# Replanning the hand-written engine order of a fused RWKV-6 attention and squared-ReLU feed-forward kernel

## The chip, the cores and the metric

The kernel runs on one core of one Trainium2 chip. A core has five engines that run side by side, each with its own queue of instructions that it takes strictly in order: TensorE (PE, matrix multiplications; its weight loads are shown apart, as PEld), VectorE (DVE), ScalarE (ACT), GpSimd (POOL) and SyncE (SP), which here only issues transfers to 16 DMA engines. Engines wait for each other by semaphores. The metric is the device time of one execution in microseconds; smaller is better.

## The reference

The inputs are r, k, v and w for 4 batches, 8 heads, 768 positions and 48 channels in float32, a vector u per head, and two matrices w_in (384 x 2048) and w_out (2048 x 384). For each batch and head a 48 x 48 state is carried over the positions, and the result goes through a feed-forward layer with a squared ReLU:

```
for t in range(S):
    cur = np.einsum('bhd,bhe->bhde', u[None] * kt, vt)
    y[:, :, t] = np.einsum('bhd,bhde->bhe', rt, state + cur)
    state = wt[:, :, :, None] * state + np.einsum('bhd,bhe->bhde', kt, vt)
x = np.ascontiguousarray(attn_out.transpose(0, 2, 1, 3)).reshape(B * S, H * D)
h = x @ w_in
r = np.maximum(h, 0.0)
g = r * r
return (g @ w_out).astype(np.float32)
```

## The kernel before

The recurrence is done in chunks of 128 positions: 4 batches of 6 chunks make 24 *steps*. Two steps (256 tokens) make a *block* of the feed-forward layer, of which there are 12. Every piece of work is a small function, and a text of *words*, `order`, says in which sequence the functions are called. The scheduler is told to leave all five engines alone (`tc.manual_schedule` at the end), so the sequence of the words is the sequence of instructions on each engine: a word that waits holds up every later word of its engine, and the relative place of words on different engines matters only through their data.

The words, with the step (or block) as the first number:

- SP: `ld:s:w`, `ld:s:k`, `ld:s:r`, `ld:s:v` load 192 KB each of a step (L67); `ld:h:I` and `ld:h:O` load slice h of w_in (L90) and of w_out (L96), eight slices of 384 KB each; `store:i:mt` stores 128 rows of the result (L345). Eight DMA semaphores are used in turn, and a transfer waits for the one eight places before it. A load also waits until its buffer is free: each of w, v and the pair r, k has seven buffers.
- ScalarE: `lw` takes the logarithm of w, `exp` (L197, or L199 and L200) exponentiates the cumulated sums, `rw` is a reciprocal of w, `v` casts v, `ac` gives the decay over a chunk, `xt` copies the transposed result into `xT`, `rl:i:g` is the ReLU of one m1 word (L321), `os` the scaled copy of a finished output tile (L341).
- VectorE: `rd` (L207) multiplies r and k by the decays, `rkt` (L220) copies their transposes, `pm` (L239) and `pmh` (L247) mask the scores, `ts` (L269) adds to the state, `q` reduces (L180), `ysb` (L291) adds up y, `gt:i:q` (L329) squares two relu tiles.
- POOL: `ku`, `qp`, `vq`, `kw`, `sn`, products of the recurrence (L172, L176, L184, L164, L273).
- TensorE: `cum` (L190) cumulates the logarithms, `tr` (L216) transposes, `p` (L234) makes the scores of one step or of two, `su` (L255 to L260) the state update, `y` (L281, L286) the output, `yt` (L297) its transposes. `m1:i:g:b` (L312) is 6 matmuls of 256 columns of x times slice g of w_in into bank b. `m2:i:mt:q:b` (L336) is 4 matmuls of 384 columns with slices 2q and 2q+1 of w_out. `warm:n:b` (L363) is n matmuls whose result nobody reads, fillers. `last` (L351) is half of the last output tile.
- `cast:i:g:j` and `cast:o:g:j` (L104) cast slice 2g+j of w_in or w_out to bfloat16, on ScalarE where g is even and on VectorE where it is odd. So w_in slices 6 and 7 are cast on VectorE (`cast:i:3:0`, `cast:i:3:1`), and m1 words with g = 7 need slice 7.

PSUM gives four banks to m1, m2, the second step's scores and the fillers (b is 0 to 3), two to `cp`, one to `tr` and one to `y`. A word that takes a bank waits until the bank's last reader is done: `rl` for m1, `os` for m2, `pmh` for scores.

Of the kernel before, what the change touches and what calls it, by code (L numbers as in the profile page):

```python
# [16 lines left out]
def kernel(  # L17
# [110 lines left out]
    warm = consts.tile([C, 512], BF16)  # L128
# [236 lines left out]
    def ld_(n, x):  # L365
# [15 lines left out]
        rd:4 m1:0:3:2 xt:3 ld:6:I m1:0:1:0 kw:5 rl:0:3 ld:7:I cum:5 tr:4 exp:5 gt:0:1 ld:0:O m1:1:0:3 ld:1:O sn:3 rkt:4
        ld:2:O m1:1:2:1 v:4 ld:3:O q:4 rl:0:1 m1:1:3:2 ld:4:O rd:5 vq:4 ld:5:O rl:1:2 m1:1:1:0 ld:5:v cast:i:2:0 su:4
        gt:0:0 p:4 ac:4 cast:i:2:1 m1:0:4:1 rl:1:3 ts:4 m1:1:4:2 cast:i:3:0 pm:4 sn:4 tr:5 rl:1:0 warm:1:3 qp:5 ld:6:w
        rl:1:4 rkt:5 m1:1:5:3 rl:1:1 y:4 gt:1:1 p:5 rl:1:5 cast:i:3:1 m1:1:6:2 cast:o:0:0 gt:1:0 m1:1:7:0 rl:0:4 gt:1:2
        m1:0:6:3 rl:1:6 cast:o:0:1 m1:0:5:1 rl:0:6 ysb:4 m1:0:7:2 rl:0:5 pm:5 ld:6:O yt:4 m2:0:1:0:3 rl:1:7 m2:0:0:0:1
        cast:o:1:0 cast:o:1:1 ld:7:O m2:1:1:0:0 gt:0:2 cast:o:2:0 m2:1:1:1:0 ld:6:k q:5 m2:0:1:1:3 cast:o:2:1 v:5 ld:7:w
        vq:5 xt:4 y:5 m2:0:1:2:3 rl:0:7 ysb:5 ld:6:r lw:6 m2:1:1:2:0 gt:0:3 rw:6 yt:5 cum:6 gt:1:3 m2:0:0:1:1 xt:5
        cast:o:3:0 m2:0:0:2:1 ld:7:k m1:2:0:2 exp:6 cast:o:3:1 ku:6 m2:1:1:3:0 ld:7:r rl:2:0 m2:0:0:3:1 kw:6 lw:7 ld:6:v
        m2:0:1:3:3 rw:7 os:0:0 rd:6 m1:2:4:2 ld:8:k os:1:1 ku:7 os:0:1 cum:7 ld:8:w tr:6 exp:7 m1:2:5:1 rkt:6 kw:7
        ld:9:w m1:2:1:0 v:6 qp:7 m2:1:0:0:3 rd:7 ld:7:v rl:2:1 qp:6 q:7 rl:2:4 tr:7 ld:8:r m1:2:6:0 rl:2:5 rkt:7 ku:8  # L390
        ld:8:v p:6 lw:8 q:6 m1:2:2:2 pm:6 vq:6 ld:9:k su:6 m1:2:3:1 ac:6 rw:8 vq:7 ld:9:r ts:6 m2:1:0:1:3 rl:2:2 gt:2:0
        p:7 v:7 ld:10:k sn:6 m1:2:7:2 pm:7 lw:9 y:6 qp:8 rl:2:6 m2:1:0:2:3 ld:11:k rl:2:3 ysb:6 m2:1:0:3:3 kw:8 ld:10:r
# [12 lines left out]
        m2:4:1:0:3 ld:16:v pmh:11:1 rw:15 ld:15:r sn:10 cum:13 y:10 v:11 pmh:11:0 m2:4:0:0:1 rw:14 ku:14 rkt:12 rl:4:7
        m2:4:1:1:3 store:1:0 ysb:10 qp:13 ld:17:v v:12 m2:4:0:1:1 exp:13 ld:16:r yt:10 gt:4:3 y:11 m2:4:1:2:3 ku:15
        xt:10 ysb:11 ld:17:r m2:4:0:2:1 rd:13 kw:14 yt:11 m2:4:1:3:3 xt:11 q:13 ld:16:w kw:15 cum:14 v:13 su:12 q:12
        m2:4:0:3:1 ac:12 ld:17:w exp:14 qp:15 ts:12 m1:5:2:0 ld:18:k tr:13 os:4:1 qp:14 rd:14 m1:5:4:2 os:4:0 store:2:1
        rl:5:2 rkt:13 m1:5:0:3 vq:13 store:2:0 ld:18:w p:12:1:0 sn:12 rl:5:0 store:4:0 su:13 rl:5:4 ld:19:w pm:12
        m1:5:3:3 vq:12 ld:18:r ac:13 lw:16 m1:5:1:2 ku:16 rl:5:3 ts:13 y:12 cum:15 pmh:13:1 rw:16 tr:14 sn:13 v:14  # L410
        m1:5:6:3 ld:19:k ysb:12 rl:5:1 kw:16 m1:5:5:0 rkt:14 pmh:13:0 yt:12 m1:5:7:2 ld:20:w xt:12 gt:5:0 y:13 exp:15
        su:14 store:4:1 gt:5:1 m2:5:1:0:1 ld:19:r ac:14 ysb:13 rl:5:6 m2:5:1:1:1 ld:20:r ts:14 rl:5:5 m2:5:0:0:3 rd:15
        sn:14 rl:5:7 yt:13 m2:5:0:1:3 xt:13 gt:5:3 cum:16 lw:18 tr:15 gt:5:2 exp:16 m1:6:0:0 q:14 m1:6:2:2 v:15 rkt:15
        qp:16 m2:5:1:2:1 rl:6:0 rd:16 m2:5:1:3:1 rl:6:2 vq:14 su:15 q:15 lw:17 p:14:0:2 ku:17 os:5:1 q:16 m2:5:0:2:3
        ac:15 store:5:1 pmh:15:0 lw:19 ku:18 ld:20:k m2:5:0:3:3 rw:17 pm:14 ld:21:r m1:6:1:1 v:16 kw:17 ld:18:v os:5:0
        m1:6:3:0 ts:15 rl:6:1 qp:17 y:14 rl:6:3 ld:19:v m1:6:4:3 ysb:14 vq:15 cum:17 pmh:15:1 tr:16 rl:6:4 ld:21:w ku:19
        m1:6:5:1 exp:17 rkt:16 y:15 store:3:0 gt:6:0 yt:14 ld:22:w rl:6:5 m1:6:6:0 sn:15 ysb:15 ld:23:w xt:14 m1:6:7:2
        rd:17 qp:18 yt:15 m2:6:0:0:3 ld:21:k xt:15 gt:6:1 cum:18 rl:6:6 su:16 gt:6:2 m1:7:2:1 ac:16 rw:18 ld:20:v q:18
        m1:7:3:0 rl:6:7 kw:18 ts:16 m2:6:0:1:3 ld:22:k rl:7:2 gt:6:3 m1:7:0:2 exp:18 store:5:0 q:17 tr:17 ld:21:v
        m2:6:0:2:3 rw:19 qp:19 rd:18 ld:23:k rl:7:3 m1:7:1:1 rkt:17 kw:19 rl:7:0 m2:6:0:3:3 ld:22:r rl:7:1 gt:7:1  # L420
        p:16:0:2 os:6:0 sn:16 m1:7:6:1 pm:16 lw:21 ld:22:v vq:16 tr:18 rl:7:6 m1:7:4:3 ld:23:r gt:7:0 cum:19 vq:17
        m1:7:7:1 rl:7:4 pmh:17:1 v:17 y:16 vq:18 m1:7:5:3 v:18 ysb:16 ku:21 lw:20 m2:7:0:0:2 pmh:17:0 rl:7:5 m2:7:0:1:2
        rkt:18 ku:20 exp:19 m2:6:1:0:0 gt:7:2 yt:16 m2:6:1:1:0 qp:20 xt:16 rd:19 m2:7:1:0:3 rw:21 kw:21 su:18 y:17 ac:18
        cum:20 rl:7:7 m2:7:1:1:3 ysb:17 lw:22 ts:18 m2:7:1:2:3 rw:20 gt:7:3 yt:17 v:20 m2:7:0:2:2 sn:18 q:20 xt:17
        m2:6:1:2:0 q:19 kw:20 exp:20 tr:19 m2:6:1:3:0 rkt:19 vq:19 m2:7:1:3:3 os:6:1 rd:20 qp:21 m2:7:0:3:2 v:19
        store:6:1 ld:23:v os:7:1 p:18:1:0 ku:22 q:21 os:7:0 m1:8:0:3 pm:18 store:7:0 m1:8:2:2 store:6:0 rl:8:0 su:19
        pmh:19:1 m1:8:6:3 ac:19 rl:8:2 ts:19 y:18 cum:21 pmh:19:0 m1:8:3:0 exp:21 ysb:18 tr:20 m1:8:1:2 rl:8:3 rkt:20
        y:19 rw:22 gt:8:1 yt:18 m1:8:7:1 rl:8:6 kw:22 ysb:19 xt:18 m1:8:4:0 rd:21 rl:8:1 sn:19 yt:19 m1:8:5:3 xt:19
        gt:8:0 cum:22 rl:8:4 su:20 m1:9:0:2 ac:20 rl:8:5 ts:20 m2:8:0:0:0 exp:22 gt:8:2 m1:9:1:3 sn:20 tr:21 rl:8:7
# [48 lines left out]
```

## Time and profile before

| what | value |
|---|---|
| median of 6 runs | 194.89 us (193.75 to 195.54) |
| the profiled execution | 194.91 us, span 193.0 us |
| PE busy | 184.1 us (95% of the span) |
| DVE, ACT, POOL busy | 144.2, 132.2, 110.7 us |
| DMA | 30.20 MB, q1 67.2% of 16 engines' span |
| loads, median from issue to landing | 3.7 to 3.9 us (w, k, r, v), 5.6 and 7.0 us (w_in, w_out) |

The span runs from the first to the last instruction; what lies around it makes up the rest of the execution's time. The second part of the page cuts the span into 40 slices and gives the busy share of each in tenths, with the granted TensorE clock:

```profile
PE   6899789899999999999999999999999999999993
PEclk9999999999999999999999999999999999999999
DMA  6999998999999979997898959990050000004032
```

The DMA engines are full from the first microseconds to beyond the middle, and nearly still in the last quarter. TensorE has gaps in the first quarter and at the very end only. A busy share of TensorE counts filler matmuls too, so the first quarter has to be looked at by line.

### The profile page before, as it was taken

The page shows a single profiled execution, that of the slowest core. Times are in us where ns is not written, and L with a number is a line of the kernel's source. Part 1 is how long each engine was busy: PE and PEld are TensorE (multiplying, and loading weights), DVE is VectorE, ACT ScalarE, POOL GpSimd, SP SyncE. Part 2 cuts the span into 40 slices and gives each one's busy share as a digit, 9 for nine tenths or more (in the row PEclk, how much of TensorE's full clock was granted, in tenths as well). Part 3 has the DMA queues.
Part 4 walks back from the last instruction along what each step waited for, and adds up shares of the span by engine and source line. Part 5 has one row for each costly group of instructions (what it writes and reads, how often), then busy time and mean ns, then how long its engine had stood idle before and what let it go on. Part 6 is the DMA issues. An engine that isn't in the chain of part 4 may idle for free.

```text
span 193.0 us, 4976 instructions
## 1 busy us (share of the span) xinstructions
PE 184.1 (95%) x1962; PEld 136.7 (71%) x1966; DVE 144.2 (75%) x211; ACT 132.2 (68%) x284; POOL 110.7 (57%) x128
## 2 busy tenths in 40 slices
PE   6899789899999999999999999999999999999993
PEld 2355548676687787787688787886688787688763
DVE  3586987895679889789979959988888858744310
ACT  3554379788777876899487876877768677247530
POOL 7488556401789749949994595795905950130000
PEclk9999999999999999999999999999999999999999
DMA  6999998999999979997898959990050000004032
GB/s 122 202 208 193 288 263 234 311 332 251 197 189 195 209 156 219 179 248 157 189 238 190 202 128 211 195 198 11 11 155 0 0 3 0 5 0 163 3 122 82
DMA packets 108840, 30.20 MB, mean 156 GB/s; under 512 B 100497, under 2 KB 108818, under 8 KB 108818
## 3 DMA queue, kind: packets, MB, share of 16 engines
q1 hardware_dynamic: 108818, 29.89, 67.2%
q8 instruction: 15, 0.25, 0.5%
q14 instruction: 7, 0.06, 0.1%
HBM read 25.17 MB, written 4.72 MB: 155 GB/s over the span
## 4 chain that ended last, share of the span: by engine, by line
PE 77%; SPq 14%; DMA 3%; DVE 2%; issue 2%; DVEq 0%
PE mm L336 31%; PE mm L312 28%; SPq L67 11%; PE tr L216 4%; SPq L90 4%; DMA w_st<-in_moe_w_in_dram 3%; PE y L281 2%; PE cp L234 2%; PE tr L297 2%; PE cp L190 2%; PE y L286 1%; PE tr L255 1%; PE mm L351 1%; PE mm L234 1%; PE tr L260 1%
## 5 line engine op out<-in xcount | busy, mean ns | idle before, releaser
L312 PE MATMUL mm<-xT,wi_sb 128*128 128x256 bf16 x576 | 73.9, 273 | 0.8 <-ACT rl L321 0.5
L336 PE MATMUL mm<-wo_sb,gt 128*128 128x384 bf16 x368 | 68.3, 326 | 0.0
L321 ACT ACTIVATE rl<-mm 128x512 f16<-128x512 f32 x96 | 55.0, 598 | 18.8 <-PE mm L312 15.5
L312 PEld LDWEIGHTS <-wi_sb 128*128 128x128 bf16 x576 | 53.8, 98 | 10.3 <-issue 1.0
L336 PEld LDWEIGHTS <-gt 128*128 128x128 bf16 x368 | 34.6, 98 | 18.1
L329 DVE TENSOR_TENSOR gt<-rl 128x1024 bf16<-128x1024 f16 x48 | 38.7, 819 | 8.6 <-ACT rl L321 8.6
L184 POOL TENSOR_TENSOR vq<-v_raw,q 128x384 f32<-128x384 f32 x24 | 21.6, 905 | 17.6 <-DVE q L180 17.6
L172 POOL TENSOR_TENSOR ku<-rk_raw,u_bc 128x384 f32<-128x384 f32 x24 | 25.6, 1070 | 8.4 <-DMA rk_raw<-in_k_dram 5.0
L164 POOL TENSOR_TENSOR rk_raw<-rk_raw,rw 128x384 f32<-128x384 f32 x19 | 19.3, 1019 | 15.6 <-ACT rw L160 12.4
L207 DVE TENSOR_TENSOR rdec_buf<-rk_raw,cp 128x768 bf16<-128x768 f32 x24 | 22.8, 948 | 6.1 <-ACT cp L197 2.9
L273 POOL TENSOR_TENSOR S<-t_state,a_c 128x384 bf16<-128x384 f32 x20 | 18.1, 907 | 15.5 <-DVE t_state L269 13.7
L176 POOL TENSOR_TENSOR qprod<-rk_raw,ku 128x384 f32<-128x384 f32 x24 | 25.2, 1057 | 2.6 <-DVE q L180 1.8
L220 DVE COPY rkT<-tr 128x1024 bf16<-128x1024 bf16 x24 | 16.5, 687 | 10.0 <-PE tr L216 9.7
L239 DVE TENSOR_TENSOR pmT<-cp,tri_strict 128x1024 bf16<-128x1024 f32 x16 | 19.5, 1218 | 1.5 <-PE cp L234 1.5
L291 DVE TENSOR_TENSOR y_sb<-vq,y 128x384 bf16<-128x384 f32 x24 | 13.2, 550 | 8.5 <-PE y L286 4.7
L300 ACT COPY xT<-tr 128x384 bf16<-128x384 bf16 x24 | 11.5, 481 | 11.1 <-PE tr L297 10.9
L156 ACT ACTIVATE lw_buf<-w_raw 128x384 bf16<-128x384 f32 x24 | 12.6, 524 | 5.0 <-DMA w_raw<-in_w_dram 5.0
L363 PE MATMUL mm<-warm 128*128 128x512 bf16 x47 | 14.2, 411 | 1.5 <-DVE warm L129 1.3
L216 PE MATMUL tr<-ident,rdec_buf 128*128 128x128 bf16 x192 | 14.6, 219 | 0.1
L341 ACT ACTIVATE o_sb<-mm 128x384 f32<-128x384 f32 x23 | 11.0, 492 | 5.1 <-PE mm L336 4.9
L216 PEld LDWEIGHTS <-rdec_buf 128*128 128x128 bf16 x192 | 12.6, 98 | 2.5 <-issue 0.7
L168 ACT CAST v_bf<-v_raw 128x384 bf16<-128x384 f32 x24 | 12.0, 508 | 2.4 <-DMA v_raw<-in_v_dram 2.4
(59 smaller groups left out, 197.4 us busy)
## 6 DMA issues: line engine op xcount, KB each, us to landing
w_raw<-in_w_dram SPq DMA_DIRECT2D x24, 192.0 KB, 3.8
rk_raw<-in_k_dram SPq DMA_DIRECT2D x24, 192.0 KB, 3.7
rk_raw<-in_r_dram SPq DMA_DIRECT2D x24, 192.0 KB, 3.9
v_raw<-in_v_dram SPq DMA_DIRECT2D x24, 192.0 KB, 3.9
out_dram<-o_sb SPq DMA_DIRECT2D x23, 192.0 KB, 2.7
w_st<-in_moe_w_in_dram SPq DMA_DIRECT2D x8, 384.0 KB, 5.6
w_st<-in_moe_w_out_dram SPq DMA_DIRECT2D x8, 384.0 KB, 7.0
out_dram<-o_sb SPq DMA_DIRECT2D x2, 96.0 KB, 1.6
```

The lines of the kernel that those rows point to most:

```text
L67: nc.sync.dma_start(out=dst, in_=src[b, :, c * C:(c + 1) * C, :].rearrange("h c d -> c h d"))
L164: nc.gpsimd.tensor_mul(k_s, k_s, tiles.pop(("rw", s))[:])
L172: nc.gpsimd.tensor_mul(ku[:], raw["rk", s][:, 1], u_bc[:])
L176: nc.gpsimd.tensor_mul(qp[:], raw["rk", s][:, 0], tiles.pop(("ku", s))[:])
L184: nc.gpsimd.tensor_mul(vq[:], raw["v", s][:], tiles.pop(("q", s))[:, :, None].to_broadcast([C, H, D]))
L207: nc.vector.tensor_mul(rdec[:, :, :, 0:D], raw["rk", s][:], tiles.pop(("cs", s))[:, :, 0:DM].rearrange("p a (h d) -> p a h d", h=H))
L216: nc.tensor.transpose(ps_tr[:, i, p, :], rdec[:, i, 2 * p:2 * p + 2, :], ident[:])
L239: nc.vector.tensor_mul(pmT[:].rearrange("p e a t -> p (e a) t"), tiles.pop(("p", s))[:].rearrange("p e (a t) -> p (e a) t", a=HP), tri_str ...
L312: nc.tensor.matmul(ps1[:, j * width:(j + 1) * width], wi_sb[:, kk, n * 128:(n + 1) * 128], xT[:, kk, s0 * C:s0 * C + width], start=(kk == ...
L321: nc.scalar.activation(tiles["rl", i, q][:, j], tiles.pop(("m1", i, g))[:], AF.Relu, scale=RS)
L329: nc.vector.tensor_mul(tiles["gt", i][:, 4 * q:4 * q + 4, :].rearrange("p a b -> p (a b)"), rl, rl)
L336: nc.tensor.matmul(tiles["m2", i, mt][:, 0:DM], gt[:, n, mt * 128:(mt + 1) * 128], wo_sb[:, n, :], start=(n == 0), stop=(n == NT - 1))
```

## The change

The text `order` is replaced. No function, tile, buffer count or instruction changes, apart from bank numbers. Every word of before is there again, except fillers: 17 filler words with 51 matmuls become 15 with 43. The words stand in another sequence on all five engines. Its description names a model with measured loads and a smaller DMA ring; neither a load time nor a ring size is written in the code, they belong to the planner that made the order. What the diff looks like, cut to the beginning, the stretch where step 19's w is loaded and used, and the end:

```diff
--- before.py
+++ after.py
@@ -370,75 +370,75 @@
     order = """
-        ld:0:w ld:0:k warm:6:0 ld:0:r ld:0:u ld:1:w lw:0 ld:1:k cum:0 warm:2:1 ld:1:r exp:0 ub rd:0 ld:0:v lw:1 warm:1:2
-        ld:2:w uc cum:1 ku:0 tr:0 ld:2:r exp:1 warm:8:3 rkt:0 qp:0 ld:1:v rd:1 v:0 ku:1 ld:2:k q:0 p:0 su:0 lw:2 vq:0
-        pm:0 ld:2:v warm:5:0 ac:0 ld:3:w ts:0 y:0 cum:2 sn:0 tr:1 exp:2 ld:3:k warm:4:1 rkt:1 qp:1 v:1 ld:4:k rd:2 su:1
-        ku:2 warm:1:2 ac:1 v:2 ld:3:r q:1 p:1 warm:2:3 ts:1 vq:1 lw:3 ld:3:v pm:1 tr:2 sn:1 warm:3:0 ld:0:I rkt:2 qp:2
-        ld:1:I cum:3 warm:3:1 exp:3 ld:2:I ysb:0 ku:3 ld:4:w yt:0 y:1 rd:3 ld:4:r xt:0 warm:1:2 qp:3 su:2 ysb:1 v:3 p:2
-        warm:3:3 ac:2 ts:2 q:3 yt:1 warm:2:0 xt:1 ld:5:w pm:2 vq:3 cast:i:0:0 tr:3 warm:1:1 sn:2 rkt:3 y:2 q:2 p:3
-        ld:3:I su:3 cast:i:1:0 vq:2 ld:5:k pm:3 m1:0:0:2 ld:4:I ac:3 ku:4 m1:0:2:3 lw:4 ts:3 rl:0:0 cum:4 ld:4:v ysb:2
-        qp:4 warm:2:0 exp:4 y:3 cast:i:0:1 yt:2 rl:0:2 ld:5:r warm:6:1 ysb:3 lw:5 ld:5:I xt:2 cast:i:1:1 rw:5 yt:3 ku:5
-        rd:4 m1:0:3:2 xt:3 ld:6:I m1:0:1:0 kw:5 rl:0:3 ld:7:I cum:5 tr:4 exp:5 gt:0:1 ld:0:O m1:1:0:3 ld:1:O sn:3 rkt:4
-        ld:2:O m1:1:2:1 v:4 ld:3:O q:4 rl:0:1 m1:1:3:2 ld:4:O rd:5 vq:4 ld:5:O rl:1:2 m1:1:1:0 ld:5:v cast:i:2:0 su:4
-        gt:0:0 p:4 ac:4 cast:i:2:1 m1:0:4:1 rl:1:3 ts:4 m1:1:4:2 cast:i:3:0 pm:4 sn:4 tr:5 rl:1:0 warm:1:3 qp:5 ld:6:w
-        rl:1:4 rkt:5 m1:1:5:3 rl:1:1 y:4 gt:1:1 p:5 rl:1:5 cast:i:3:1 m1:1:6:2 cast:o:0:0 gt:1:0 m1:1:7:0 rl:0:4 gt:1:2
-        m1:0:6:3 rl:1:6 cast:o:0:1 m1:0:5:1 rl:0:6 ysb:4 m1:0:7:2 rl:0:5 pm:5 ld:6:O yt:4 m2:0:1:0:3 rl:1:7 m2:0:0:0:1
...
-        rl:5:2 rkt:13 m1:5:0:3 vq:13 store:2:0 ld:18:w p:12:1:0 sn:12 rl:5:0 store:4:0 su:13 rl:5:4 ld:19:w pm:12
...
-        ac:15 store:5:1 pmh:15:0 lw:19 ku:18 ld:20:k m2:5:0:3:3 rw:17 pm:14 ld:21:r m1:6:1:1 v:16 kw:17 ld:18:v os:5:0
-        m1:6:3:0 ts:15 rl:6:1 qp:17 y:14 rl:6:3 ld:19:v m1:6:4:3 ysb:14 vq:15 cum:17 pmh:15:1 tr:16 rl:6:4 ld:21:w ku:19
-        m1:6:5:1 exp:17 rkt:16 y:15 store:3:0 gt:6:0 yt:14 ld:22:w rl:6:5 m1:6:6:0 sn:15 ysb:15 ld:23:w xt:14 m1:6:7:2
-        rd:17 qp:18 yt:15 m2:6:0:0:3 ld:21:k xt:15 gt:6:1 cum:18 rl:6:6 su:16 gt:6:2 m1:7:2:1 ac:16 rw:18 ld:20:v q:18
...
-        m1:11:0:0 gt:10:3 rl:11:2 m2:10:0:0:3 rl:11:0 m2:10:0:1:3 m1:11:1:1 m2:10:0:2:3 rl:11:1 m1:11:5:0 gt:11:0
-        m1:11:3:1 rl:11:5 m2:10:0:3:3 rl:11:3 gt:11:2 m2:11:0:0:0 os:10:0 gt:11:1 m2:10:1:2:2 store:10:0 m2:10:1:3:2
-        m2:11:0:1:0 os:10:1 m2:11:0:2:0 store:10:1 store:8:1 m2:11:0:3:0 os:11:0 store:11:0 last:11:1:1:0 last:11:1:2:1
+        ld:0:w ld:0:k warm:6:0 ld:0:u ld:0:r ld:1:w lw:0 ld:0:v cum:0 ld:1:r ub exp:0 ld:1:k warm:2:1 rd:0 lw:1 ld:2:w
+        tr:0 uc cum:1 rkt:0 ld:1:v v:0 ku:0 warm:1:2 exp:1 su:0 ld:2:k warm:8:3 ac:0 rd:1 ku:1 ld:2:r lw:2 ts:0 ld:0:I
+        qp:1 p:0 tr:1 pm:0 v:1 ld:2:v qp:0 warm:3:0 rkt:1 ld:3:w cum:2 sn:0 warm:1:1 exp:2 q:1 su:1 ku:2 warm:6:2 ld:3:r
+        ac:1 rd:2 vq:1 ld:3:k q:0 p:1 warm:2:3 ts:1 vq:0 ld:1:I pm:1 tr:2 qp:2 y:0 lw:3 ld:4:w warm:2:0 v:2 rkt:2 cum:3
+        ld:5:w warm:3:1 exp:3 ysb:0 ku:3 q:2 yt:0 y:1 ld:3:v xt:0 rd:3 warm:1:2 sn:1 su:2 ld:2:I ac:2 ysb:1 p:2
+        cast:i:0:0 qp:3 warm:2:3 ts:2 ld:4:k pm:2 yt:1 vq:2 warm:2:0 xt:1 ld:3:I lw:4 tr:3 ld:4:v sn:2 q:3 m1:0:0:1 lw:5
+        rkt:3 vq:3 v:3 y:2 rl:0:0 p:3 cast:i:0:1 ld:4:r su:3 pm:3 cast:i:1:0 m1:0:1:2 ku:4 ld:5:k rl:0:1 m1:0:2:3 ysb:2
+        ac:3 cum:4 rw:5 ts:3 ld:5:r y:3 exp:4 cast:i:1:1 yt:2 warm:1:0 sn:3 ld:4:I ysb:3 m1:0:3:1 xt:2 v:4 yt:3 rd:4
+        qp:4 ld:5:I warm:3:2 xt:3 ld:6:I rl:0:2 ld:7:I ku:5 cum:5 q:4 tr:4 ld:0:O rl:0:3 ld:1:O m1:1:0:0 gt:0:0 exp:5
+        ld:2:O m1:1:2:2 kw:5 ld:3:O rkt:4 ld:5:v m1:1:3:3 rl:1:2 gt:0:1 su:4 qp:5 cast:i:2:0 m1:1:1:1 rd:5 ac:4 m1:1:4:2
+        vq:4 rl:1:3 ts:4 p:4 rl:1:0 cast:i:2:1 m1:0:4:3 sn:4 rl:1:1 pm:4 ld:4:O tr:5 cast:i:3:0 ld:5:O m1:1:5:0 gt:1:1
+        ld:6:w rl:0:4 m1:0:6:1 gt:1:0 rl:1:4 y:4 m1:0:5:3 rl:1:5 rkt:5 m1:1:6:2 cast:i:3:1 rl:0:5 ysb:4 rl:0:6 m1:0:7:0
+        cast:o:0:1 cast:o:0:0 m1:1:7:3 gt:1:2 p:5 rl:0:7 m2:1:1:0:1 ld:6:O gt:0:2 cast:o:1:0 ld:7:O yt:4 cast:o:1:1
+        m2:0:0:0:0 ld:7:w rl:1:6 q:5 m2:1:1:1:1 v:5 pm:5 vq:5 m2:0:1:0:2 cast:o:2:0 m2:0:1:1:2 ld:6:k rl:1:7 y:5
+        cast:o:2:1 m2:0:0:1:0 xt:4 ysb:5 ld:6:r m2:0:0:2:0 lw:6 gt:1:3 rw:6 yt:5 cum:6 m2:1:1:2:1 xt:5 gt:0:3 cast:o:3:0
...
+        rkt:14 exp:15 sn:13 ld:20:v pmh:13:1 yt:12 ld:19:k m1:5:7:0 store:4:1 xt:12 gt:5:0 y:13 store:2:0 rl:5:5 su:14
+        gt:5:1 ld:21:v m2:5:1:0:2 ac:14 ld:20:k v:15 ts:14 m2:5:0:0:1 rl:5:6 ysb:13 ld:19:w m2:5:1:1:2 rw:16 rd:15 yt:13
+        kw:16 m2:5:0:1:1 xt:13 cum:16 rl:5:7 gt:5:2 tr:15 ld:18:r qp:16 m1:6:2:3 exp:16 rkt:15 m1:6:0:0 ld:20:w qp:17
+        rl:6:2 rd:16 m2:5:1:2:2 rl:6:0 store:4:0 sn:14 su:15 q:16 m2:5:0:2:1 ac:15 v:16 gt:5:3 p:14:3:0 vq:15 lw:18
+        ts:15 m2:5:0:3:1 rw:18 pm:14 sn:15 rw:17 m2:5:1:3:2 lw:19 tr:16 kw:17 pmh:15:0 os:5:1 y:14 os:5:0 cum:17
...
+        m1:11:3:1 os:10:1 m1:11:0:3 rl:11:3 m1:11:4:0 rl:11:0 gt:11:1 m1:11:1:1 m1:11:5:3 rl:11:1 m2:10:0:3:2 rl:11:4
+        gt:11:0 m1:11:6:1 rl:11:5 m1:11:7:0 os:10:0 gt:11:2 rl:11:6 store:10:0 m2:11:0:0:3 rl:11:7 m2:11:0:1:3 gt:11:3
+        m2:11:0:2:3 m2:11:0:3:3 os:11:0 store:11:0 store:10:1 last:11:1:2:0 last:11:1:0:1
```

## The prediction

> **What bounds the kernel now.** I read four views in this order: the busy time by stage, the waits of TensorE, the chain of work that ended last, and the timelines of VectorE and ScalarE around the place where the chain leaves the DMA. First the stages (columns: stretch and length, then busy us and count for PE, PEld, DVE, ACT, POOL, then clock, DMA share, GB/s), and below them the same first stretch for the filler matmuls of L363 alone (PE, PEld, clock, DMA share, GB/s):
>
> ```profile
> 0.00:40.30 40.30, 34.68 (x341) 21.38 (x345) 29.80 (x45) 24.15 (x46) 24.40 (x40) 1.00 0.96 234
> 40.30:190.40 150.10, 149.41 (x1621) 115.31 (x1621) 114.45 (x167) 108.06 (x238) 86.30 (x88) 1.00 0.61 138
> ...
> 0.00:40.30 40.30, 14.23 (x47) 4.73 (x51) 1.00 0.96 234
> ```
>
> From 40.3 us TensorE has work without a break: 149.41 of 150.10 us. Before that it is busy for 34.68 us, but 14.23 of them are fillers, so some 20 us of 40 are useful, while the DMA engines are 96% busy. The kernel is DMA-bound to 40 us and TensorE-bound after. The useful TensorE work is the same in both orders, so the end moves only by (a) how much of it is done, and when, as the second stage begins, and (b) waits inside the second stage. The waits that the trace names for TensorE are small (us in total, times, longest):
>
> ```profile
> PE cp L234 <- DVE rdec_buf L207: 1.2, 2, 1.1
> PE tr L297 <- ACT xT L300: 0.5, 1, 0.5
> ...
> PE mm L312 <- DVE wi_sb L104: 0.3, 1, 0.3
> ```
>
> From the timeline's start times in the second stage one `m1` word takes 0.655 us, `m2` 0.650, `tr` 0.447, `y` 0.37, `su` 0.30, `p` of one step 0.23, `yt` 0.167, `cum` 0.162. Adding these from 48 us to the end leaves 1.9 us of waits, 0.6 of them at the two `yt` words at 117.6 and 119.5, the rest in pieces under 0.2. So (b) can give at most 1.9 us back. The handover between the stages is in the chain (start, us, what):
>
> ```profile
> 29.95 6.15 DMA w_st<-in_moe_w_in_dram
> 36.27 0.73 issue
> 37.00 1.22 DVE pmT L239
> 38.22 0.61 DVE rkT L220
> 38.87 0.41 PE cp L234 x8
> 39.33 0.95 DVE wi_sb L104
> 40.33 2.79 PE mm L312 x24
> ```
>
> Slice 6 of w_in (`ld:6:I`) is issued at 29.95 and lands at 36.1; then VectorE's own order decides when slice 7, which landed at 37.2, is cast:
>
> ```profile
> 36.13 0.95 DVE L104 CAST wi_sb<-w_st 128x768 bf16<-128x768 f32 x1 [0.79 <-DMA w_st<-in_moe_w_in_dram]
> 37.00 1.22 DVE L239 TENSOR_TENSOR pmT<-cp,tri_strict 128x1024 bf16<-128x1024 f32 x1
> 38.13 0.68 DVE L220 COPY rkT<-tr 128x1024 bf16<-128x1024 bf16 x1
> 38.73 0.68 DVE L329 TENSOR_TENSOR gt<-rl 128x1024 bf16<-128x1024 f16 x1
> 39.33 0.94 DVE L104 CAST wi_sb<-w_st 128x768 bf16<-128x768 f32 x1
> ```
>
> VectorE idled 0.79 us before the cast of slice 6, and did `pm:4` (1.13 us start to start) between the casts.
>
> **Part 1, loads up to slice 7.** On both sides the same 32 transfers stand up to `ld:7:I` (w, k, r of steps 0 to 5, v of 0 to 4, u, eight slices), on a DMA that is full. So slices 6 and 7 are again 31st and 32nd and land at 36.1 and 37.2: gain 0. Inside, slices 0 and 1 come earlier (19th and 20th to 13th and 18th), v of step 3 later (18th to 21st). In before the 18th landed at 19.6 and the 21st at 23.7; I take 23.3 for v3, since one slice fewer stands ahead. `v:3` now holds up on ScalarE `rl:0:0` and `cast:i:0:1`, and `su:3` on TensorE. Walking on with the rows' durations: `v:3` to 23.8, `rl:0:0` (0.6) to 24.5, the cast (0.83) to 25.4, so `m1:0:1` starts at 25.5, the next m1 word at 26.2, `yt:2` at 27.4, `yt:3` at 28.9, `m1:1:0` at 30.5, where before it started at 31.35. It then runs with short waits to 36.35, where it waits 0.7 us for the cast of slice 6. That wait covers up to 0.7 us of error in the walk; past it each us late costs one.
>
> **Part 2, TensorE's order before slice 7.** Before, 12 `m1` words and `p:5` precede the word that waits for slice 7; after, 14 `m1` words do, and `p:5` follows. That is 2 x 0.655 - 0.23 = 1.08 us more done: **-1.08**. Room: 0:6, y:4, 0:5, 1:6 from 37.1 take 2.3 us, to 39.4, still before slice 7 is cast.
>
> **Part 3, VectorE's order.** `pm:4` goes ahead of the cast of slice 6 into the 0.79 us of idling and a bit before it (its input `p:4` ends at about 34.3, so it runs 34.4 to 35.6); between the casts now stand `gt:1:1`, `gt:1:0`, `rkt:5`. In starts: 36.13, 37.00, 37.60, 38.20, 38.80, cast done 39.74 instead of 40.27: **-0.53**.
>
> **Part 4, ScalarE's order.** Before, `cast:o:0:0` ran at 38.83. After, both casts for the first `m2` word stand behind `rl:0:5` and `rl:0:6`: m1:0:5 starts at 38.05, its relu about 0.95 later, then 0.49 + 0.49 + 0.80 + 0.80 = done at 41.6. TensorE is ready at 39.80 + 1.31 + 0.23 = 41.35: **+0.3**. The casts of w_out slices 4 and 5 land one place later (v of step 5 goes ahead): 45.06, cast at 45.95, needed at 46.1, no loss. At `m1:2:0` both orders have done the same: 49.68 before, about 48.4 after, **lead 1.3 us**.
>
> **Part 5, fillers.** 51 become 43, all in the first stage, 8 x 0.216 = 1.7 us. They stand where TensorE would wait for a load, so 0. A rule speaks against this: the Trainium skill, "TensorE: Matmul & The Clock Gate" (Part 1 and its rules on dropped throughput), says that the array starts at half clock and falls back after about 3.4 us of idling. The trace shows the first half: the first fillers (columns: start, us)
>
> ```profile
> 1.32 2.74 PE L363 MATMUL mm<-warm 128*128 128x512 bf16 x6 [1.32 <-DVE warm L129]
> ...
> 7.94 1.89 PE L363 MATMUL mm<-warm 128*128 128x512 bf16 x8
> ```
>
> start 427 ns apart, those at 7.94 only 216 ns. By the rule, if the fillers were what holds the clock, some 7 us of work between 25 and 36 us would take twice as long: +7, less about 3 us of idling, +4. By the trace the longest stretch without a matmul was 1.2 us and the granted clock stayed at 1.00; my walk has none over 1.2 us after. I take 0, and 2 in 100 for the rest.
>
> **Part 6, the second stage.** No word is added or removed; each `rl`, `gt`, `exp` is only placed elsewhere. At 117 to 120 us `yt:15` stood 1.85 us of work behind `y:15`, and waited; after, 0.37 + 0.655 + 0.167 + 1.31 = 2.5 us stand between: the 0.6 us go. New waits of like size are likely elsewhere, so I take half: **-0.3**, ends -1.9 and +3. Loads past SP's queue: r of step 8 goes from 53rd to 57th, landing by place at 62.9; `rd:8`, which started at 63.33, is needed at about 63.3: 0.4 us spare. POOL's multiplications are off the path there. **Tail:** `store:10:1` moves behind `store:11:0`; with the lead it is issued near 186.8 and lands by its median of 2.7 us at 189.5, while the last half store is issued at about 188.8. They share the DMA for 0.7 us: I take 0, at most +0.3.
>
> **Sum** against the profiled execution's own time, 194.91 us with a span of 193.0: -1.08 - 0.53 + 0.3 - 0.3 = -1.6, so a span of 191.4 and a time of **193.3**; the median of the runs, 194.89, is the same base.
>
> **Rivals.**
> *R1, slower: w of step 19 comes late.* It moves from 100th to 107th transfer, and `lw:19` stands on ScalarE ahead of `os:5:1`, which frees the bank of `m1:6:1`. By work that word is due at 113.2, so w must land by 111.9. The 106th landed at 110.9, so about 111.9: no spare. Six places ahead `ld:20:v` waits on SP for `vq:14`, on POOL behind `ku:17`, which waits for k of step 17. For it: SP did stand 4.1 us at a store before the 107th transfer of before, which so landed at 114.0. Against: that store is elsewhere now. If SP stands 4.1 us again, w lands at 116: +4.1 - 1.6, time 197.4. It decides from a landing after 114.5 (1.6 + 0.97 beyond 111.9). Chance 0.13.
> *R2, nothing left.* v of step 3 lands 2 us later than taken and the lead of 1.3 goes (0.7 covered), or new waits in the second stage eat it: time about 194.7. For it: the second stage has only 1.9 us of waits now, so a plan has more to lose there than to win. Chance 0.22.
> *R3, more.* The lead holds and most of the 1.9 us of waits go too: 194.9 - 1.3 - 1.6 = 192.0. Against: the pieces under 0.2 us are at word boundaries in any order. Chance 0.20.
> *That it does nothing:* the order is taken literally on all five queues, so it acts; but no ring size stands in the code, so nothing of the transfers' own speed changes.
>
> **How the numbers follow.** The forecast has 0.45, own range 192.6 to 194.1. A measurement here tells 0.5%, 0.97 us, from no change: the bounds are 193.9 and 195.9. Faster: 0.38 of the forecast, all of R3, 0.04 of R2 = 0.62. Slower: 0.12 of R1 and 0.02 of the clock and R2 = 0.14. The rest is 0.24. The range leaves out the far half of R1 and a little of R3: 191.6 to 195.9.
>
> **What would show it.** Right: the word for slice 7 starts near 39.8, `m1:2:0` near 48.4, the last matmul some 1.6 us before 190.0, no fall of the clock. Part 1 is wrong if no wait for slice 6 is left near 36 us; R1 shows as an L312 wait for ScalarE's L341 near 113 us; Part 6 is wrong if TensorE's busy share after 40 us falls under 99%.

## The result, and the profile after

| what | before | after |
|---|---|---|
| median, runs side by side on one chip | 195.25 us (193.75 to 197.43, 64 runs) | 194.28 us (192.61 to 197.23, 29 runs) |
| ratio after to before, 95% interval | | 0.9936 [0.9917, 0.9955] |
| the profiled execution | 194.91 us, span 193.0 | 194.28 us, span 192.5 |

The changed kernel is 0.64% faster, by 0.45 to 0.83. The forecast was 1.6 us of 194.9, 0.82%. The time of 194.28 lies a whole microsecond above the forecast of 193.3, outside the forecast's own range (192.6 to 194.1) and inside the wide one (191.6 to 195.9). But before itself ran 0.36 us above its first median beside it, so the ratio is the number to compare. Run once more later, the same kernel gave 0.9921 [0.9897, 0.9944]. Executions over 1.5% above the fastest of their kernel are left out of all ratios, means and counts of executions here and below.

First the stages of the changed kernel, cut where the word for slice 7 starts (columns as before: stretch and length, busy us and count of PE, PEld, DVE, ACT, POOL, then clock, DMA share, GB/s; the last row is the fillers of L363 alone):

```profile
0.00:40.30 40.30, 36.77 (x338) 22.34 (x341) 29.80 (x46) 23.73 (x47) 25.07 (x40) 1.00 0.99 244
40.30:189.90 149.60, 148.50 (x1617) 114.58 (x1617) 113.06 (x167) 108.78 (x238) 88.81 (x88) 1.00 0.60 135
...
0.00:40.30 40.30, 14.17 (x40) 4.14 (x43) 1.00 0.99 244
```

Without the fillers TensorE is busy for 36.77 - 14.17 = 22.6 us of the first 40.3, where before it was 20.45. Not all of the 2.15 us between them is more work: the weight loads without fillers are 298 against 294, which is two `m1` words more (12) and `p:5` less (8). The two words are 1.3 us. The rest is work that ran slower: before 12 us `tr:0`, for example, took 1.06 us, against 0.61 in before at the same place, while the clock column shows 1.00 for both. No run tells whether that costs anything. The DMA is a little fuller than it was (0.99 against 0.96). The second stage is nearly as tight as before (99.3% of it busy, against 99.5%). Next the waits that the trace names for TensorE (us in total, times, longest):

```profile
PE mm L312 <- DVE wi_sb L104: 1.1, 3, 0.6
PE mm L336 <- DVE wo_sb L104: 0.6, 1, 0.6
```

The second row is new: it is the word `m2:1:1:3`, the first that needs slices 6 and 7 of w_out. There is no L312 wait for ScalarE's L341 near 113 us, and no wait at the `yt` words near 118 us. Then TensorE around the handover, before (the first two lines) and changed (the last three). In both, the first line starts with the word for slice 7 and the last with `m1:2:0`, of which three and six matmuls fall into the stretch shown:

```profile
40.33 2.79 PE L312 MATMUL mm<-xT,wi_sb 128*128 128x256 bf16 x24 [0.30 <-DVE wi_sb L104]
49.68 0.49 PE L312 MATMUL mm<-xT,wi_sb 128*128 128x256 bf16 x3
...
40.40 1.48 PE L312 MATMUL mm<-xT,wi_sb 128*128 128x256 bf16 x12 [0.15 <-DVE wi_sb L104]
42.22 0.81 PE L336 MATMUL mm<-wo_sb,gt 128*128 128x384 bf16 x4
48.94 0.82 PE L312 MATMUL mm<-xT,wi_sb 128*128 128x256 bf16 x6
```

The word for slice 7 starts 0.07 us later than before. From it to `m1:2:0` TensorE needs 9.35 us before and 8.54 after: two `m1` words fewer are left to do. That is 0.81 us.

Last the place where the two orders differ most, VectorE at the handover (start, us, group, and in brackets the idling ahead of it and what ended it):

```profile
35.60 1.23 DVE L239 TENSOR_TENSOR pmT<-cp,tri_strict 128x1024 bf16<-128x1024 f32 x1 [0.62 <-PE cp L234]
36.74 0.94 DVE L104 CAST wi_sb<-w_st 128x768 bf16<-128x768 f32 x1
37.60 1.28 DVE L329 TENSOR_TENSOR gt<-rl 128x1024 bf16<-128x1024 f16 x2
38.80 0.69 DVE L220 COPY rkT<-tr 128x1024 bf16<-128x1024 bf16 x1
39.40 0.94 DVE L104 CAST wi_sb<-w_st 128x768 bf16<-128x768 f32 x1
```

`pm:4` now stands ahead of both casts, as the order says. But VectorE waits 0.62 us for it, while slice 6 has been in SBUF since 34.6. The second cast ends at 40.34, not earlier than the 40.27 of before. Yet `m1:2:0` starts at 48.94 instead of 49.68: 0.74 us of lead in this execution. The rest of its account: 0.7 us given back at `m2:1:1:3` (by start times; the wait itself is 0.55), 0.6 us won at the `yt` words, which makes 0.64, and the span is 0.5 us shorter.

### The profile page after: what moved, and what is told of

Read it like the earlier page. It is cut to its first block, busy times and chain, and to the rows that moved or that the text cites. A ratio compares the mean times of both kernels' runs of the same rounds, so it can differ in the third digit from the quotient of the medians.

```text
span 192.5 us, 4952 instructions
## 1 busy us (share of the span) xinstructions
PE 185.3 (96%) x1955; PEld 136.9 (71%) x1958; DVE 142.9 (74%) x211; ACT 132.5 (69%) x284; POOL 113.9 (59%) x128
## 4 chain that ended last, share of the span: by engine, by line
PE 87%; DVE 7%; ACT 2%; DMA 2%; issue 1%; DVEq 0%; ACTq 0%
PE mm L312 31%; PE mm L336 30%; PE tr L216 6%; PE mm L363 4%; PE cp L234 3%; PE y L281 2%; PE cp L190 2%; PE tr L297 2%; PE tr L255 2%; PE y L286 2%; DMA w_raw<-in_w_dram 2%; DVE wi_sb L104 1%; PE mm L351 1%; DVE wo_sb L104 1%; DVE gt L329 1%
## 5 line engine op out<-in xcount | busy, mean ns | idle before, releaser
L312 PE MATMUL mm<-xT,wi_sb 128*128 128x256 bf16 x576 | 72.7, 273 | 1.5 <-DVE wi_sb L104 1.1
L336 PE MATMUL mm<-wo_sb,gt 128*128 128x384 bf16 x368 | 69.3, 326 | 0.6 <-DVE wo_sb L104 0.6
L312 PEld LDWEIGHTS <-wi_sb 128*128 128x128 bf16 x576 | 53.8, 98 | 10.8 <-DVE wi_sb L104 2.2
L329 DVE TENSOR_TENSOR gt<-rl 128x1024 bf16<-128x1024 f16 x48 | 37.0, 786 | 9.1 <-ACT rl L321 9.0
L164 POOL TENSOR_TENSOR rk_raw<-rk_raw,rw 128x384 f32<-128x384 f32 x19 | 21.1, 1111 | 17.5 <-ACT rw L160 14.4
L172 POOL TENSOR_TENSOR ku<-rk_raw,u_bc 128x384 f32<-128x384 f32 x24 | 26.5, 1108 | 8.0 <-DMA rk_raw<-in_k_dram 4.3
L176 POOL TENSOR_TENSOR qprod<-rk_raw,ku 128x384 f32<-128x384 f32 x24 | 25.9, 1082 | 1.4 <-DVE q L180 1.1
L341 ACT ACTIVATE o_sb<-mm 128x384 f32<-128x384 f32 x23 | 11.1, 491 | 11.2 <-PE mm L336 11.2
L363 PE MATMUL mm<-warm 128*128 128x512 bf16 x40 | 14.2, 473 | 1.4 <-DVE warm L129 1.3
L216 PE MATMUL tr<-ident,rdec_buf 128*128 128x128 bf16 x192 | 15.1, 223 | 0.1
L180 DVE TENSOR_REDUCE q<-qprod 128x8 f32<-128x384 f32 x24 | 13.0, 543 | 0.0
```

The costliest lines, as they stand in the source:

```text
L164: nc.gpsimd.tensor_mul(k_s, k_s, tiles.pop(("rw", s))[:])
L172: nc.gpsimd.tensor_mul(ku[:], raw["rk", s][:, 1], u_bc[:])
L176: nc.gpsimd.tensor_mul(qp[:], raw["rk", s][:, 0], tiles.pop(("ku", s))[:])
L216: nc.tensor.transpose(ps_tr[:, i, p, :], rdec[:, i, 2 * p:2 * p + 2, :], ident[:])
L312: nc.tensor.matmul(ps1[:, j * width:(j + 1) * width], wi_sb[:, kk, n * 128:(n + 1) * 128], xT[:, kk, s0 * C:s0 * C + width], start=(kk == ...
L329: nc.vector.tensor_mul(tiles["gt", i][:, 4 * q:4 * q + 4, :].rearrange("p a b -> p (a b)"), rl, rl)
```

## The experiments

The theory was the prediction's: the gain is made in the first stage, by two more `m1` words ahead of slice 7 and an earlier cast, and a smaller part at `yt:15`. Its rivals were that the profiled lead is only an earlier landing of the slices in one execution, and that the second stage's new order does the work. Where differences in us are given, they are between the means over the executions of a kernel and of before on the same chip, with a 95% interval.

**The order cut in two at `m1:2:0`.** At that word TensorE has done the same in both orders, so each half can be joined to the other's. `h_new_old` takes the changed order to there and the old one from there; the two loads `ld:7:r` and `ld:7:k` are put so that each appears once, and banks are renamed at the joint.

```diff
-        ld:0:w ld:0:k warm:6:0 ld:0:r ld:0:u ld:1:w
+        ld:0:w ld:0:k warm:6:0 ld:0:u ld:0:r ld:1:w
...
-        xt:5 cast:o:3:0 m2:0:0:2:1 ld:7:k m1:2:0:2 exp:6 cast:o:3:1 ku:6 m2:1:1:3:0 ld:7:r rl:2:0
+        xt:5 gt:0:3 cast:o:3:0 m2:0:1:2:2 ld:7:r ld:7:k m1:2:0:3 exp:6 cast:o:3:1 ku:6 m2:1:1:3:1 rl:2:0
...
```

> The new order up to the word m1:2:0, the old order after it (banks renamed so that they fit). Theory A, the gain is made before m1:2:0 (there the changed kernel's profile leads by 0.74 us): the time keeps most of the gain, about 0.7 us below before, and with the old second stage's 0.6 us of waits at 117 to 120 us still in it. Rival B, the gain is made in the second stage (the waits at 117 to 120 us are gone): the time is that of before within 0.3 us.

> New order up to m1:2:0, old after it, once more to narrow the split. The first time it ran 0.9 us below before, where the changed kernel ran 1.5 us below. Theory, each half of the run carries about half of the gain: 0.6 to 1.1 us below before again. Rival, nearly all is the first stage: 1.2 us or more below. Rival, nearly all is the second: under 0.4 us below.

Measured: 0.9954 [0.9928, 0.9981] and, on another chip, 0.9907 [0.9878, 0.9936]; 0.89 and 1.70 us faster, pooled 1.27 +/- 0.30. The opposite half, `h_old_new`, has the old order to `m1:2:0` and the changed one after it:

```diff
-        ld:0:w ld:0:k warm:6:0 ld:0:u ld:0:r ld:1:w
+        ld:0:w ld:0:k warm:6:0 ld:0:r ld:0:u ld:1:w
...
-        xt:5 gt:0:3 cast:o:3:0 m2:0:1:2:2 ld:7:r m1:2:0:3 exp:6 cast:o:3:1 ld:7:k m2:1:1:3:1 lw:7 m2:0:1:3:2 ku:6
+        xt:5 cast:o:3:0 m2:0:0:2:1 ld:7:k ld:7:r m1:2:0:2 exp:6 cast:o:3:1 m2:1:1:3:0 lw:7 m2:0:1:3:3 ku:6
...
```

> The old order up to m1:2:0, the new order after it. Theory A: about before, or 0.5 us below it at most. Rival B: the whole gain, 1.0 to 1.3 us below before. In both theories the wait of m2:1:1:3 for cast:o:3:1 is decided by where the second stage's start puts POOL's ku:6.

> Old order up to m1:2:0, new after it, once more. The first time 0.8 us below before. Theory of halves: 0.5 to 1.1 us below again. Rival, first stage: under 0.3 us below. Rival, second stage: 1.2 us or more below.

Measured: 0.9953 [0.9921, 0.9984] and 0.9972 [0.9945, 0.9999]; 0.80 and 0.64 us, pooled 0.71 +/- 0.36. Both halves gain, about two thirds in the first stage and one third in the second. The profile of the first `h_new_old` shows one way in which an execution loses its lead. Two stretches of it (columns as above):

```profile
26.00:28.00 2.00, 0.74 (x8) 0.43 (x6) 1.48 (x4) 1.08 (x3) 0.78 (x1) 0.99 0.71 150
28.00:30.00 2.00, 2.00 (x20) 1.47 (x19) 1.33 (x3) 0.56 (x1) 1.27 (x3) 0.50 0.73 149
```

A slice came late (VectorE idled 0.52 us for it), TensorE stood 1.26 us for the cast, and the granted clock fell to half for about 3 us. `m1:2:0` came at 50.49 in that execution, against 48.10 in the profile of the second run. This does not explain why the first run gained less than the second: without its 4 executions (of 22) at a lowered clock it gains 1.05 us, still not 1.70. That difference stays open.

**The same two kernels again.** Is the earlier landing of slices 6 and 7 in the profile of after (34.6 and 35.7, against 36.1 and 37.2) a property of the order? The changed kernel and before were run again, with no edit.

> The changed kernel as it is, for a second profile. Theory, slice 6 lands earlier than in before because the new order of the loads feeds the DMA better: it lands at 34.6 again, within 0.3 us. Rival, where it lands varies from execution to execution: it lands anywhere between 34.5 and 36.2.

> Before as it is, for a second profile. Theory: slice 6 lands at 36.1 again, within 0.3 us. Rival: anywhere between 34.5 and 36.2 us; and cast:i:3:1 then ends 0.2 us from 40.3 or earlier by as much as slice 6.

Measured: the changed kernel 194.05 us, 0.9921 [0.9897, 0.9944]; before 195.44 us in one execution, where the runs beside it have a median of 195.42. Slice 6 landed at 34.6 in the changed kernel, and at 35.3 in before. Over all profiles it landed between 34.6 and 36.95 with the changed order of loads, and between 34.1 and 36.1 with the old one. So the landing varies by more than 2 us between executions of either order, and is not what the change brings. Nor is the start of the word for slice 7 steady: between 39.7 and 40.3 with the old first stage, between 39.4 and 40.4 with the new one, and 41.95 where the clock fell. What is steady is the stretch from that word to `m1:2:0`: 9.34 or 9.35 us in four of the five profiles with the old first stage (the fifth has 10.38, with a wait of 0.89 for ScalarE in it), and 8.48 to 8.54 in eight of the nine with the new one (the ninth, `e_cast_o` below, has a wait of its own). So 0.81 us is in every execution. `m1:2:0` itself starts at 49.68, 49.50, 50.10, 49.61 and 49.66 with the old first stage, and at 48.94, 48.15, 48.10 and, where the clock fell, 50.49 with the new one and its fillers: 1.3 us earlier on average without the last, 0.8 with it.

The repeat also told something of the new wait. In the changed kernel's second profile it was absent, and before, which didn't have it in its first profile, had it in its second, with 0.71 us. VectorE's casts of w_out slices 6 and 7 in the first profile of the changed kernel:

```profile
47.95 2.62 DVE L104 CAST wo_sb<-w_st 128x768 bf16<-128x768 f32 x2
```

and POOL beside them:

```profile
47.56 1.33 POOL L172 TENSOR_TENSOR ku<-rk_raw,u_bc 128x384 f32<-128x384 f32 x1 [3.24 <-DMA rk_raw<-in_k_dram]
48.97 1.19 POOL L164 TENSOR_TENSOR rk_raw<-rk_raw,rw 128x384 f32<-128x384 f32 x1
```

The same two casts in its second profile, where POOL's `ku:6` began only at 48.26, after them:

```profile
47.16 1.02 DVE L104 CAST wo_sb<-w_st 128x768 bf16<-128x768 f32 x2
```

Two casts take 1.02 us alone and 2.62 us beside POOL. The wait at `m2:1:1:3` occurs with both orders, so the order alone doesn't make it; in these profiles it goes with the time at which k of step 6 lands and lets `ku:6` begin.

**`pm:4` moved back.** If VectorE's wait for `p:4` ahead of the cast of slice 6 costs time, the cast should go first. The edit in the changed kernel:

```diff
-        rl:1:1 pm:4 ld:4:O tr:5 cast:i:3:0 ld:5:O m1:1:5:0 gt:1:1 ld:6:w
+        rl:1:1 ld:4:O tr:5 cast:i:3:0 ld:5:O m1:1:5:0 gt:1:1 pm:4 ld:6:w
```

> The changed kernel with one word moved: pm:4 goes behind cast:i:3:0 and gt:1:1. Theory, slice 6 landed at 34.6 and waited 2.1 us for VectorE, which stood before pm:4 for p:4: cast:i:3:0 starts near 35.0, cast:i:3:1 ends near 38.6 instead of 40.35, the two waits of m1 words before slices 6 and 7 (0.5 and 0.3 us) go, m1:2:0 starts 0.7 to 0.9 us earlier, time -0.7 us against the changed kernel. Rival, the DMA or ScalarE's relu takes over (rl:1:4 behind gt:1:1, casts of w_out): under -0.2 us.

> The changed kernel with pm:4 behind cast:i:3:0 and gt:1:1, once more, since the first time gave six executions only. Theory, VectorE's order costs the changed kernel 0.5 us or more before slice 7: time 0.5 to 0.9 us below the changed kernel, 2.0 us or more below before. Rival, when slices 6 and 7 land decides, and that varies by more than this: within 0.3 us of the changed kernel, about 1.5 us below before.

Measured: 0.9874 [0.9822, 0.9926] from only 6 runs, then 0.9935 [0.9913, 0.9957] from 22. The larger sample is the changed kernel's own value, and the pooled gain over before, 1.53 +/- 0.35 us, is that of `again_new`, 1.54 +/- 0.37. TensorE in the second profile shows where it went (start, us, group, wait):

```profile
39.16 0.37 PE L281 MATMUL y<-v_bf,pmT 128*128 128x48 bf16 x8 [0.90 <-DVE pmT L239]
```

`y:4` is the next to need `pm:4`; with the mask later, TensorE waits there. In this execution the slice too came late (VectorE idled 0.78 us for it), so moving `pm:4` back gave the first cast nothing to run on. And what the first cast can win, the second loses: with `pm:4` between them it starts 3.80 us after the first in all profiles with this move, and 2.66 without it. No gain or loss from the place of `pm:4` is seen, and one under some 0.4 us would not be.

**The casts of w_out earlier.** To take the new wait away, the two casts go ahead of POOL's `ku:6` and `kw:6`, in the changed kernel:

```diff
-        v:5 pm:5 vq:5
+        v:5 pm:5 cast:o:3:0 vq:5
...
-        lw:6 gt:1:3
+        lw:6 cast:o:3:1 gt:1:3
...
-        gt:0:3 cast:o:3:0 m2:0:1:2:2
+        gt:0:3 m2:0:1:2:2
...
-        exp:6 cast:o:3:1 ld:7:k
+        exp:6 ld:7:k
```

> The changed kernel with cast:o:3:0 moved behind pm:5 and cast:o:3:1 ahead of gt:1:3 on VectorE, to where POOL stands still. Theory, the casts took 1.36 us each because POOL's ku:6 and kw:6 ran beside them: they take 0.55 us, the 0.55 us wait of m2:1:1:3 goes, time -0.5 us against the changed kernel. Rival, the casts took long because their data had just landed or because of the DMA: they stay at 1.3 us, and ysb:5 and yt:5 come later, time 0 to +0.5 us.

Measured: 0.9931 [0.9894, 0.9969]. The wait at `m2:1:1:3` is gone and the casts take 0.56 us each. The first does so though its slice has only just landed, which rules out the rival that fresh data makes these casts slow. But VectorE now stands for the transfer:

```profile
46.61 0.56 DVE L104 CAST wo_sb<-w_st 128x768 bf16<-128x768 f32 x1 [3.06 <-DMA w_st<-in_moe_w_out_dram]
```

`ysb:5` is queued behind it, and TensorE waits 1.2 us for it at `yt:5`. One wait took the place of another. A second try joined the later place of `pm:4` with both casts just behind `ysb:5`:

```diff
-        rl:1:1 pm:4 ld:4:O
+        rl:1:1 ld:4:O
...
-        gt:1:1 ld:6:w
+        gt:1:1 pm:4 ld:6:w
...
-        ysb:5 ld:6:r
+        ysb:5 cast:o:3:0 cast:o:3:1 ld:6:r
...
-        gt:0:3 cast:o:3:0 m2:0:1:2:2
+        gt:0:3 m2:0:1:2:2
...
-        exp:6 cast:o:3:1 ld:7:k
+        exp:6 ld:7:k
```

> The changed kernel with pm:4 behind cast:i:3:0 and gt:1:1, and cast:o:3:0 and cast:o:3:1 moved up to just behind ysb:5. Theory, VectorE's places of these casts are what TensorE waits for at 37 to 51 us: the waits before slices 6 and 7 and of m2:1:1:3 (together 1.5 us in the profile of the changed kernel) shrink under 0.6 us, time 0.8 to 1.2 us below the changed kernel. Rival, the transfers of slices 6 and 7 of w_in and w_out hold instead: no more than 0.3 us below.

Measured: 194.45 us, 0.9929 [0.9902, 0.9956]. The casts take 0.55 us and `m2:1:1:3` waits no longer, but `y:4` waits 0.90 us. Again no more than the changed kernel.

**Most fillers taken out.** Of the changed kernel's 43 fillers, 8 are left (the first two words); for example:

```diff
-        ku:0 warm:1:2 exp:1 su:0 ld:2:k warm:8:3 ac:0 rd:1
+        ku:0 exp:1 su:0 ld:2:k ac:0 rd:1
...
```

> The changed kernel with 8 filler matmuls (the first two filler words) in place of 43. Theory, fillers only fill waits and the clock stays: time within 0.3 us of the changed kernel, granted clock 1.00. Rival, the clock rule: with some 7 us of fillers gone between 8 and 32 us the granted clock falls to 0.5[...] in most executions, TensorE's words there take twice as long, m1:2:0 starts 1 to 4 us later and the time is 1 to 4 us longer.

Measured: 194.13 us, 0.9927 [0.9903, 0.9951], the same as the changed kernel beside it (0.9921). The clock did fall in its profile (columns as above):

```profile
12.00:16.00 4.00, 1.72 (x20) 1.18 (x20) 3.59 (x7) 0.88 (x2) 3.51 (x5) 0.67 1.03 236
16.00:20.00 4.00, 3.69 (x43) 2.91 (x44) 3.74 (x7) 2.12 (x4) 2.54 (x4) 0.50 1.05 244
```

TensorE at half clock was still fast enough in this execution, since the stage waits for the DMA (share 1.03 and 1.05); `m1:2:0` came at 47.63, the earliest of all profiles. The mean clock was below 0.995 in 9 of its 17 executions, and these were on average 0.2 us longer than the others (194.09 against 193.87), with an interval of 0.7 on either side.

**The second stage's part alone.** In the kernel before, only `gt:6:0` is moved behind `ysb:15`:

```diff
-        y:15 store:3:0 gt:6:0 yt:14 ld:22:w rl:6:5 m1:6:6:0 sn:15 ysb:15 ld:23:w
+        y:15 store:3:0 yt:14 ld:22:w rl:6:5 m1:6:6:0 sn:15 ysb:15 gt:6:0 ld:23:w
```

> Before with one word moved: gt:6:0 goes behind ysb:15 on VectorE. Theory, the wait of 0.55 us at the yt words at 117 to 120 us is VectorE's gt:6:0 (1.48 us beside POOL's sn:15 and qp:18) standing ahead of ysb:15, and it is what the second stage of the new order saves: both waits go in the profile and the time is 0.4 to 0.7 us below before. Rival, the saved wait turns up at the next word (rl:6:6 and gt:6:1 come later), or the second stage's gain is made elsewhere: under 0.2 us.

Measured: 0.9966 [0.9937, 0.9994], 0.6 us faster. VectorE in before, where the square stands ahead of the sum that `yt:15` waits for:

```profile
117.51 1.48 DVE L329 TENSOR_TENSOR gt<-rl 128x1024 bf16<-128x1024 f16 x1
118.91 0.54 DVE L291 TENSOR_TENSOR y_sb<-vq,y 128x384 bf16<-128x384 f32 x1
```

and with the one word moved:

```profile
118.99 0.56 DVE L291 TENSOR_TENSOR y_sb<-vq,y 128x384 bf16<-128x384 f32 x1 [0.16 <-issue]
119.46 0.78 DVE L329 TENSOR_TENSOR gt<-rl 128x1024 bf16<-128x1024 f16 x1
```

The start of the sum isn't earlier on the clock of this execution, which was 1.25 us behind at `y:15` (it had a wait of 1.1 us at `m2:1:1:3`). But it starts 0.63 us after `y:15` and not 1.80, so `y_sb` is there by the time `yt:15` is reached, and its wait of 0.4 us is gone; the 0.15 us at `yt:14` stay. This one move agrees in size with the whole second half of the change (0.71 +/- 0.36). That fits the move being all of it, and does not prove it.

## Why the prediction was right, point by point

The direction, the size within the interval and the likeliest course held. The steps did so unequally, and that the total fits is in part luck: Part 3's 0.53 us is not to be seen in the profiles, and Part 6 gave more than twice its size. The two halves add up to 1.98 us, while the whole change measured 1.2 to 1.5, so the split itself is known to some 0.4 us only.

- **Part 1, the loads.** That the order of loads gains nothing held: slices 6 and 7 vary by more between executions than between the orders. The walk came out about 1 us early in the first profile (`m1:1:0` was put at 30.5 and started at 31.49), and within 0.2 in the repeat (30.70). Its step "the next m1 word at 26.2" failed in both: that word starts 1.48 us after `m1:0:1`, at 27.62 and 26.83, and not 0.7. `cast:i:1:0`, its input, stands on VectorE behind `pm:3`, which idled 0.67 us for `p:3` on TensorE. The walk had followed ScalarE and TensorE there, and not VectorE's own queue. The rest of the first profile's microsecond isn't steady: `m1:0:1`, put at 25.5, started at 26.14 and at 25.35. The wait of 0.7 us, said to cover an error in the walk, did so.
- **Part 2, TensorE's order, -1.08.** Held: 14 `m1` words precede the word for slice 7, `p:5` follows it, and the first stage alone gains 1.27 +/- 0.30 us. The sum is a little high: `p:5` took 0.33 us to the next word (38.87 to 39.20 before), not 0.23, which makes 0.98.
- **Part 3, VectorE's order, -0.53.** Its mechanism failed in the first profile: `p:4` started at 35.16 and not near 34.1 (the microsecond of Part 1), so `pm:4` didn't fall into idle time but made some, and the second cast ended at 40.34 instead of 39.74. In the repeat everything was 0.8 us earlier, and it ended at 39.56; before's repeat had 39.97. Between the two casts the 0.53 is there (2.66 us from start to start, against 3.20), but the first cast now waits for `pm:4`. A single profile can't tell 0.5 us here, and `e_pm4_2` gives no sign that the gain comes from the place of `pm:4`.
- **Part 4, ScalarE's casts, +0.3.** Held, with its mechanism: the first `m2` word starts 0.05 us after ScalarE's second cast ends (42.17 and 42.22, and likewise in all nine profiles with the new first stage). Parts 2 and 4 together were put at 0.78 us, and 0.81 was measured between the word for slice 7 and `m1:2:0`.
- **The lead of 1.3 us at `m1:2:0`.** Right over executions (1.27 +/- 0.30); the one profile of after shows 0.74. Of it 0.81 us is steady, from Parts 2 and 4. Where the remaining 0.46 +/- 0.30 comes from no profile settles: an earlier word for slice 7, as Part 3 had it, shows in some and not in others. The signs came late in the first profile: 40.40 and 48.94 us, put near 39.8 and 48.4, and 39.61 and 48.15 in the repeat.
- **Part 5, fillers, 0.** The time was right, the reason only half. I took the clock to hold because no stretch without a matmul was longer than 1.2 us. In `h_new_old` it fell after a stretch of 1.26, and in `e_few_fillers` after stretches of 1.11 and 0.71. The rule of the Trainium skill ("TensorE: Matmul & The Clock Gate", Part 1), that the clock follows how busy the array has lately been, fits these falls (TensorE was busy for 0.74 of the 2 us up to the first, and for 1.72 of the 4 us around the second); its idle time of some 3.4 us isn't needed for it, since no stretch was that long. But the price of +4 was far too high. Of 128 executions with the changed first stage and its fillers, 11 had a mean clock below 0.995, and these averaged 195.02 us against 193.85: 1.2 us. Not all of that need be the clock's: in the profile of `h_new_old` a late slice came with it. Nor is the fall the new order's: before shows it in 13 of 129 executions. A fall at 13 to 20 us in `e_few_fillers` cost next to nothing.
- **Part 6, the second stage, -0.3.** Mis-sized, by little more than the interval: 0.71 +/- 0.36 us. I took half of the 0.6 us at the `yt` words, for new waits elsewhere; all of it was kept. The one new wait, at `m2:1:1:3`, lies at the boundary of the stages and occurs with the old order too.
- **R1, step 19's w late.** Its first half happened. SP in the changed kernel (start, us, issue):

```profile
97.26 0.88 SPq L67 DMA_DIRECT2D w_raw<-in_w_dram  x1
102.60 0.37 SPq L67 DMA_DIRECT2D v_raw<-in_v_dram  x1
```

The second line is `ld:20:v`, for which SP stood 4.4 us, until `vq:14` ended. Step 19's w was issued at 106.23 all the same. Its landing isn't in the trace; the transfers issued before and after it landed at 109.63 and 112.00. `lw:19` ran at 113.08 with no idling ahead of it, and TensorE waited for nothing there. So the load came in time, and how much it had to spare stays open.
- **R2 and R3.** Neither. The lead was not eaten, and the changed kernel, 1.54 +/- 0.37 us faster in its repeat, stayed well short of R3's 2.9.

Left open: what makes the landing of a slice vary by 2 us between executions of one kernel, which sets the scatter of a single profile; why the two runs of `h_new_old` differ by 0.81 +/- 0.61 us; and whether the fall of the clock near 28 us can be kept away by another place for the fillers, which wasn't tried. The two `m1` words were not moved alone, so their 0.81 us rests on the profiles and not on a run of its own. No version beat the changed kernel: `e_few_fillers`, `e_cast_o`, `e_pm4_2` and `e_pm4_casts` lie between 0.9927 and 0.9935, within its interval.

## What to carry to other kernels

While a start-up is bound by transfers, compute that is moved ahead of the last one can be gained nearly one for one (here 0.81 of 0.98 us); so count the words on each side of that transfer, and check the order of the rest only where it makes the next word late. Walk every engine's queue to the input of a moved word, and not only those on which the path was last seen: the step that failed here was a cast behind another instruction in VectorE's queue. And don't read half a microsecond from one profile of such a start-up; cut the order in two at a point where both have done the same work, and time each half.

## What the runs showed of the hardware

**VectorE beside POOL.** A cast of a w_out slice took 0.55 us alone and up to 1.36 us beside POOL's products; a square (`gt`, two inputs in SBUF) 0.68 us alone and up to 1.48; POOL's own products went from 1.00 to 1.33 us. The strided casts of w_in took 0.94 us in all cases, and the operations with an input in PSUM (`pm`, `rd`, `ts`, `ysb`) didn't change. The Trainium skill, "SBUF — State Buffer" (the section on SBUF's two separate sides), says that the two engines share one pair of ports, which a GpSimd instruction and certain VectorE instructions take for their whole length and exclude each other from; among the latter it counts those with two SBUF inputs. That agrees with these rows: in the changed kernel's first profile both casts end 0.42 us after a product of POOL does (49.31 after 48.89, 50.58 after 50.16). The profile's times on POOL are rough, and no run here shows the ports themselves. A planner that gives each operation one duration misses this.

**The clock.** The granted clock fell to half with stretches without a matmul of no more than 1.3 us, and was below 0.995 in 11 of 128 executions despite the fillers.
